# Where the tail of a matmul kernel's code lies: all supertiles inside the loop, the last emptied in halves, the last three chunks stored as one run per partition

## The chip, the cores and the metric

One core of one Trainium2 chip. The metric is the device time of one execution in microseconds (us); each kernel is executed several times, and medians are quoted with their range. The profile's span (first to last instruction) is about 1.7 us shorter than that time. All runs compared here are fast, at a granted TensorE clock of 0.995 or more.

## The reference

The depthwise kernel is 1x1, so the whole is a scale of each channel and a matrix product over 147,456 rows of 384 channels, in bf16:

```python
H = W = 384; C = 384; k = 1
out = out + xp[:, i:i+H, j:j+W, :] * dw[i, j][None, None, None, :]   # one (i, j) only
return jnp.einsum('bhwc,cd->bhwd', out, pw)                          # 384 x 384
```

## The kernel before

Rows are taken in 288 supertiles of 512. SyncE loads and stores chunks of one to ten supertiles. VectorE transposes a supertile in 32x32 blocks, TensorE multiplies it in 48 matmuls (four row tiles at a time) into one of two PSUM buffers, ScalarE empties the buffer into an output tile as bf16. The channel scale is folded into the weights at the start.

```python
head, tail = [[1, 1, 2, 2, 4]], [[6, 4], [3, 2, 1, 1, 1]]      # chunks, in supertiles
...
with nc.tensor.Fori(0, NS // 2 - 2, 1) as it:                  # 284 supertiles in the loop
    rv = nc.tensor.to_reg(it + 1)
    for s in range(2):
        supertile(s, rv)
supertile(0, NS // 2 - 1)                                      # three more as straight code
supertile(1, NS // 2 - 1)
supertile(0, NS // 2)
for ps, c0, c1 in ((1, 0, DS), (0, DS, D)):                    # the last: 256, then 128 columns
    ...                                                        # 48 matmuls each
```

So 480 instructions of straight code (matmuls with their weight loads) follow the loop. The last two supertiles are emptied by ScalarE and VectorE together, the last of them in two column parts. The two stores before the last write runs of 768 bytes; the very last store writes one run of 3072 bytes per partition:

```python
if t + 1 < NT:
    dst = of[512 * first : 512 * (first + L), :].rearrange("(q p j) d -> p q (j d)", q=4, p=P)
else:
    dst = of[512 * first :, :].rearrange("(m q) d -> m (q d)", q=4)
```

## Time and profile before

| | before |
|---|---|
| median, range | 577.61 us (577.1 to 577.85, 3 runs) |
| span of the profiled execution | 575.28 us |
| first emptying starts / last emptying is released | 9.85 / 569.56 us |
| last store issued / last landing seen by SyncE / end | 570.08 / 573.96 / 575.28 us |

TensorE sets the pace up to the last release; after that come a copy, a store and the closing of the program, 5.72 us together. I call this last stretch "release to end".

Two more views, which the prediction does not show. The first is the page's list of DMA queues (packets, MB, share of 16 engines' span); the second the SyncE queue in order of time near 512 us (start, duration of the issues, count):

```profile
q1 hardware_dynamic: 25924, 226.79, 98.0%
q8 instruction: 3, 0.05, 0.0%
q14 instruction: 9, 0.07, 0.0%
```

```profile
511.91 2.57 SPq L111 DMA_DIRECT2D X<-in_x_dram  x5
516.37 19.89 SPq L127 DMA_DIRECT2D out_dram<-O  x2
```

The DMA engines are 98% busy, and instructions travel through them too, on q8 and q14. Of the 19.89 us of the second SyncE row, the issue of one single store took 9.0 us by its record; most others take 0.33 to 0.5 us.

### The profile page before, as it was taken

The page shows a single profiled execution, that of the slowest core. Times are in us where ns is not written, and L with a number is a line of the kernel's source. Part 1 is how long each engine was busy: PE and PEld are TensorE (multiplying, and loading weights), DVE is VectorE, ACT ScalarE, POOL GpSimd, SP SyncE. Part 2 cuts the span into 40 slices and gives each one's busy share as a digit, 9 for nine tenths or more (in the row PEclk, how much of TensorE's full clock was granted, in tenths as well). Part 3 has the DMA queues.
Part 4 walks back from the last instruction along what each step waited for, and adds up shares of the span by engine and source line. Part 5 has one row for each costly group of instructions (what it writes and reads, how often), then busy time and mean ns, then how long its engine had stood idle before and what let it go on. Part 6 is the DMA issues. An engine that isn't in the chain of part 4 may idle for free.

```text
span 575.3 us, 29802 instructions
## 1 busy us (share of the span) xinstructions
PE 567.2 (99%) x13919; PEld 415.8 (72%) x13919; DVE 509.9 (89%) x584; ACT 418.2 (73%) x297; POOL 1.7 (0%) x8
## 2 busy tenths in 40 slices
PE   8999999999999999999999999999999999999995
PEld 5777777777777777777777777777777777777774
DVE  6999999999999999999999999999999999999994
ACT  6777777777777777777777777777777777777774
POOL 1000000000000000000000000000000000000000
PEclk9999999999999999999999999999999999999999
DMA  8999999999999999999999999999999999998876
GB/s 344 429 399 428 425 415 428 428 430 409 376 411 419 374 399 430 397 390 389 432 398 389 397 429 388 389 401 432 387 394 410 423 390 391 409 402 320 369 282 227
DMA packets 25938, 226.92 MB, mean 394 GB/s; under 512 B 1221, under 2 KB 5702, under 8 KB 22086
## 3 DMA queue, kind: packets, MB, share of 16 engines
q1 hardware_dynamic: 25924, 226.79, 98.0%
q8 instruction: 3, 0.05, 0.0%
q14 instruction: 9, 0.07, 0.0%
q10 hardware_dynamic: 2, 0.00, 0.0%
HBM read 113.54 MB, written 113.25 MB: 394 GB/s over the span
## 4 chain that ended last, share of the span: by engine, by line
PE 98%; ACT 0%; DVE 0%; issue 0%; POOL 0%; POOLq 0%; SPq 0%
PE ps L162 97%; PE ps L181 0%; ACT w_r L292 0%; PE ps L241 0%; DVE O L322 0%; PE ps L212 0%; POOL zero L253 0%; POOL warm L252 0%; POOLq L355 0%; PE ps L196 0%; SPq L99 0%
## 5 line engine op out<-in xcount | busy, mean ns | idle before, releaser
L162 PE MATMUL ps<-w_r,T 32*128 32x384 bf16 x13776 | 559.8, 321 | 0.9 <-ACT w_r L292 0.9
L279 DVE STREAM_TRANSPOSE T<-X 128x384 uint32<-128x384 uint32 x576 | 505.9, 879 | 54.4
L325 ACT CAST O<-ps 128x1536 bf16<-128x1536 f32 x289 | 413.0, 1429 | 148.3 <-PE ps L162 147.7
L162 PEld LDWEIGHTS ps<-w_r,T 32*128 32x128 bf16 x13776 | 411.6, 93 | 149.1 <-issue 1.2
L292 ACT CAST w_r<-ps 128x768 bf16<-128x768 f32 x5 | 3.6, 820 | 1.9 <-PE ps L212 1.9
L181 PE MATMUL ps<-zero 32*128 32x384 bf16 x32 | 2.8, 517 | 1.4 <-POOL zero L253 1.4
L322 DVE CAST O<-ps 128x768 bf16<-128x768 f32 (+2 forms) x3 | 2.1, 691 | 1.4 <-PE ps L162 1.1
L297 DVE COPY dw_f<-ps 128x3 f32<-128x3 f32 x1 | 0.2, 160 | 3.0 <-PE ps L196 3.0
L212 PE MATMUL ps<-pw_n,sel_w 128*128 128x384 bf16 x12 | 2.7, 357 | 0.0
L181 PEld LDWEIGHTS ps<-zero 32*128 32x128 bf16 x32 | 1.1, 118 | 2.0 <-issue 1.7
L212 PEld LDWEIGHTS ps<-pw_n,sel_w 128*128 128x128 bf16 x12 | 1.0, 105 | 1.9 <-issue 0.7
L265 ACT ACT_TABLE_LOAD x1 | 1.3, 1283 | 1.5 <-SPq L99 1.5
L241 PE MATMUL ps<-w_r,T 32*128 32x256 bf16 (+1 forms) x96 | 2.2, 241 | 0.0
L241 PEld LDWEIGHTS ps<-w_r,T 32*128 32x128 bf16 x96 | 2.0, 93 | 0.2
L292 DVE CAST w_r<-ps 128x768 bf16<-128x768 f32 x1 | 1.0, 956 | 1.2 <-PE ps L212 1.2
L301 DVE TENSOR_SCALAR sel_w<-sel,dw_f 128x512 bf16<-128x512 bf16 x3 | 0.9, 347 | 0.1
L255 POOL TENSOR_SCALAR_AFFINE_SELECT sel<-ones 128x512 bf16<-128x512 bf16 x1 | 0.7, 735 | 0.1
L196 PEld LDWEIGHTS ps<-ones,dw_row 1*128 1x128 bf16 x3 | 0.3, 127 | 0.3 <-issue 0.2
L254 POOL MEMSET ones<- 128x512 bf16 x1 | 0.5, 528 | 0.0
L265 ACT COPY warm<-warm 128x1 f32<-128x1 f32 x2 | 0.3, 189 | 0.0
L253 POOL MEMSET zero<- 128x192 uint32 x1 | 0.3, 258 | 0.0
L196 PE MATMUL ps<-ones,dw_row 1*128 1x1 bf16 x3 | 0.3, 174 | 0.0
(5 smaller groups left out, 0.5 us busy)
## 6 DMA issues: line engine op xcount, KB each, us to landing
X<-in_x_dram SPq DMA_DIRECT2D x26, 3840.0 KB, 21.8
out_dram<-O SPq DMA_DIRECT2D x26, 3840.0 KB, 27.8
X<-in_x_dram SPq DMA_DIRECT2D x2, 1536.0 KB, 17.5
out_dram<-O SPq DMA_DIRECT2D x2, 1536.0 KB, 14.6
X<-in_x_dram SPq DMA_DIRECT2D x3, 768.0 KB, 7.5
out_dram<-O SPq DMA_DIRECT2D x3, 768.0 KB, 9.6
X<-in_x_dram SPq DMA_DIRECT2D x1, 2304.0 KB, 19.9
out_dram<-O SPq DMA_DIRECT2D x1, 2304.0 KB, 12.8
```

Of the source, the lines that this page charges most:

```text
L162: mm = nc.tensor.matmul(PS[s][:, q, :D], lhsT=Ts[s][32 * q : 32 * q + 32, b, par::2], rhs=w_r[32 * q : 32 * q + 32, b, par, :], start=(b = ...
L181: nc.tensor.matmul(PS[0][:, i % 4, :D], lhsT=zero[32 * (i % 4) : 32 * (i % 4) + 32, 0:P], rhs=zero[32 * (i % 4) : 32 * (i % 4) + 32, :], s ...
L196: mm = nc.tensor.matmul(PS[1][:, k, D : D + 1], lhsT=dw_row[:, P * k : P * k + P], rhs=ones[0:1, 0, 0:1], start=True, stop=True,)
L212: mm = nc.tensor.matmul(w_ps(b)[:, r, :], lhsT=sel_w[:, b // 2, 2 * (b % 2) + r, :], rhs=pw_n[:, b // 2, :], start=True, stop=True,)
L241: mm = nc.tensor.matmul(PS[ps][:, q, : c1 - c0], lhsT=Ts[1][32 * q : 32 * q + 32, b, par::2], rhs=w_r[32 * q : 32 * q + 32, b, par, c0:c1] ...
L255: nc.gpsimd.affine_select(out=sel[:].rearrange("p (v r) (q w) -> p v r q w", v=2, q=4), in_=ones[:].rearrange("p (v r) (q w) -> p v r q w" ...
L265: c = nc.scalar.copy(warm[:, s + 1 : s + 2], warm[:, 0:1])
L279: ins = nc.vector.transpose(out=Tw[:, 3 * h : 3 * h + 3], in_=Xw[:, :, j, 96 * h : 96 * h + 96].rearrange("p k (b w) -> p b k w", w=32),)
L292: i = nc.vector.tensor_copy(out, in_) if e == 0 else nc.scalar.copy(out, in_)
L301: nc.vector.tensor_scalar_mul(sel_w[:, k], sel[:], dw_f[:, k : k + 1]).then_inc(s_sw)
L322: e = nc.vector.tensor_copy(Ov[:, nq:4, j, c0:c1], PS[ps][:, nq:4, : c1 - c0])
L325: a = nc.scalar.copy(Ov[:, 0:nq, j, c0:c1], PS[ps][:, 0:nq, : c1 - c0])
```

## The change

Its intent: a shorter program whose tail is the same code as its body, and longer runs in the last stores.

```diff
-            if t + 1 < NT:
+            if first + LONG < NS:                       # LONG = 3: the last three chunks
                 ...  # p-major load, 768-byte runs in the store
             else:
                 ...  # load in 768-byte runs, store in one 3072-byte run per partition
-        with nc.tensor.Fori(0, NS // 2 - 2, 1) as it:
+        with nc.tensor.Fori(0, NS // 2, 1) as it:
             rv = nc.tensor.to_reg(it + 1)
             for s in range(2):
                 supertile(s, rv)
-        supertile(0, NS // 2 - 1)
-        supertile(1, NS // 2 - 1)
-        supertile(0, NS // 2)
-        for ps, c0, c1 in ((1, 0, DS), (0, DS, D)):
-            ...
+            nq = 4
+            if jj + 1 == NS:
+                nq = 2
+                ...
+                e = nc.vector.tensor_copy(Ov[:, nq:4, j, :], PS[s][:, nq:4, :D])
+            a = nc.scalar.copy(Ov[:, 0:nq, j, :], PS[s][:, 0:nq, :D])
```

More of the change, by code (lines that the diff above doesn't have):

```diff
@@ L14 @@
 NR = 3
-DS = 256
+LONG = 3
 def _groups(n_super: int):
@@ L102, in load_x @@
             dst = Xs[g % NR][:, 4 * off : 4 * (off + L), :]
-            if t + 1 < NT:
-                src = xf[512 * first : 512 * (first + L), :].rearrange("(p s) c -> p (s c)", p=P)
+            rows = xf[512 * first : 512 * (first + L), :]
+            if first + LONG < NS:
+                src = rows.rearrange("(p s) c -> p (s c)", p=P)
                 dst = dst.rearrange("p s c -> p (s c)")
             else:
-                src = xf[512 * first :, :].rearrange("(a k q) c -> q a k c", k=4, q=4)
+                src = rows.rearrange("(a k q) c -> q a k c", k=4, q=4)
             if i == 0 and g >= NR:
@@ L116, in store @@
             src = Os[g % NR][:, 4 * off * D : 4 * (off + L) * D]
-            if t + 1 < NT:
-                dst = of[512 * first : 512 * (first + L), :].rearrange("(q p j) d -> p q (j d)", q=4, p=P)
+            rows = of[512 * first : 512 * (first + L), :]
+            if first + LONG < NS:
+                dst = rows.rearrange("(q p j) d -> p q (j d)", q=4, p=P)
                 src = src.rearrange("p (q e) -> p q e", q=4)
-                nc.sync.wait_ge(s_a[je % 2], je // 2 + 2)
-                if je >= NS - 2:
-                    nc.sync.wait_ge(s_d, 1)
-            else:
-                dst = of[512 * first :, :].rearrange("(m q) d -> m (q d)", q=4)
-                nc.sync.wait_ge(s_a[1], NS // 2 + 2)
-                nc.sync.wait_ge(s_d, 3)
+            else:
+                dst = rows.rearrange("(m q) d -> m (q d)", q=4)
+            nc.sync.wait_ge(s_a[je % 2], je // 2 + 2)
+            if je + 1 == NS:
+                nc.sync.wait_ge(s_d, 1)
             nc.sync.dma_start(dst, src).then_inc(s_o[g % NR], 16)
@@ L225 @@
                 supertile(s, rv)
-        supertile(0, NS // 2 - 1)
-        supertile(1, NS // 2 - 1)
-        supertile(0, NS // 2)
-        for ps, c0, c1 in ((1, 0, DS), (0, DS, D)):
-            for b in range(NB):
-                for par in range(2):
-                    for q in range(4):
-                        if par == 0 and q == 0:
-                            if ps == 1 and b in (0, 3):
-                                nc.tensor.wait_ge(s_t[1][b // 3], NS // 2)
-                            if b == 0:
-                                nc.tensor.wait_ge(s_a[ps], NS // 2 + (ps == 0))
-                                if ps == 0:
-                                    nc.tensor.wait_ge(s_d, 1)
-                        mm = nc.tensor.matmul(
-                            PS[ps][:, q, : c1 - c0],
-                            lhsT=Ts[1][32 * q : 32 * q + 32, b, par::2],
-                            rhs=w_r[32 * q : 32 * q + 32, b, par, c0:c1],
-                            start=(b == 0 and par == 0),
-                            stop=(b == NB - 1 and par == 1),
-                            tile_position=(32 * q, 0),
-                        )
-            mm.then_inc(s_pe)
         nc.gpsimd.memset(warm[:], 0.0).then_inc(s_seed)
@@ L312 @@
                 nc.scalar.wait_ge(s_o[g % NR], 16 * sum(map(len, groups[g % NR : g : NR])))
-            if jj + 2 < NS:
-                parts = [(s, 0, D, 4, 2 * jj + 2)]
-            elif jj + 2 == NS:
+            nq = 4
+            if jj + 1 == NS:
+                nq = 2
                 nc.vector.wait_ge(s_o[g % NR], 16 * sum(map(len, groups[g % NR : g : NR])))
-                parts = [(s, 0, D, 2, 2 * jj + 2)]
-            else:
-                parts = [(1, 0, DS, 2, 2 * jj + 1), (0, DS, D, 2, 2 * jj + 2)]
-            for ps, c0, c1, nq, v in parts:
-                if nq < 4:
-                    e = nc.vector.tensor_copy(Ov[:, nq:4, j, c0:c1], PS[ps][:, nq:4, : c1 - c0])
-                    e._wait_ge(s_pe, v)
-                    e.then_inc(s_d)
-                a = nc.scalar.copy(Ov[:, 0:nq, j, c0:c1], PS[ps][:, 0:nq, : c1 - c0])
-                a._wait_ge(s_pe, v)
-                a.then_inc(s_a[s])
+                e = nc.vector.tensor_copy(Ov[:, nq:4, j, :], PS[s][:, nq:4, :D])
+                e._wait_ge(s_pe, 2 * jj + 2)
+                e.then_inc(s_d)
+            a = nc.scalar.copy(Ov[:, 0:nq, j, :], PS[s][:, 0:nq, :D])
+            a._wait_ge(s_pe, 2 * jj + 2)
+            a.then_inc(s_a[s])
             if jj + 2 < NS:
```

## The prediction

> **What bounds the kernel now.** I read the page's busy shares first, then the chain that ended last, then the last 10 us in order of time, because the diff touches only the last five of 288 supertiles (512 rows each).
>
> ```profile
> PE 567.2 (99%) x13919; PEld 415.8 (72%) x13919; DVE 509.9 (89%) x584; ACT 418.2 (73%) x297; POOL 1.7 (0%) x8
> ...
> PE 98%; ACT 0%; DVE 0%; issue 0%; POOL 0%; POOLq 0%; SPq 0%
> ```
>
> TensorE is busy 99% of the span and carries 98% of the chain. One supertile is 48 matmuls of 384 columns. The ScalarE emptyings of consecutive supertiles start at 561.70, 563.65, 565.60 and 567.55 us in the trace: 1.95 us each, inside the loop and in the unrolled code after it alike. 288 x 1.95 = 561.6 us, and the change leaves all of it. What it can move is what lies after TensorE: 575.28 less the last release at 569.56, some 5.7 us, or 1% of the time. The timeline of that stretch (columns: start, duration, engine, line, operation, tiles, shape, count, idle before):
>
> ```profile
> 565.60 1.44 ACT L325 CAST O<-ps 128x1536 bf16<-128x1536 f32 x1 [0.51 <-PE ps L162]
> 567.07 3.35 SPq L127 DMA_DIRECT2D out_dram<-O  x3
> 567.16 2.17 PEld L241 LDWEIGHTS ps<-w_r,T 32*128 32x128 bf16 x96
> 567.32 2.19 PE L241 MATMUL ps<-w_r,T 32*128 32x256 bf16 x96
> 567.55 0.96 DVE L322 CAST O<-ps 128x768 bf16<-128x768 f32 x1 [1.07 <-PE ps L162]
> 567.55 0.80 ACT L325 CAST O<-ps 128x768 bf16<-128x768 f32 x1 [0.51 <-PE ps L162]
> 568.86 1.07 ACT L325 CAST O<-ps 128x512 bf16<-128x512 f32 x2 [0.51 <-PE ps L241]
> 568.86 1.12 DVE L322 CAST O<-ps 128x512 bf16<-128x512 f32 x2 [0.35 <-PE ps L241]
> ```
>
> The last supertile is computed as 256 and then 128 columns, so its first part is emptied (0.69 us on VectorE) while the second is computed; the second is released at 569.56 and costs another 0.42 us. The last copy ends at 569.98 and the last store is issued at 570.08. Then only DMA is left, as the SyncE queue's waits from 566 us on say:
>
> ```profile
> SPq L140 <- DMA out_dram<-O: 3.5, 1, 3.5
> ```
>
> That wait ends at 573.96; closing the program takes the other 1.31 us. The stretches after 571.5 us (sum, PE, PEld, DVE, ACT, POOL, clock, DMA share, GB/s) show how the DMA ends:
>
> ```profile
> 571.50:572.00 0.50, 0.00 (x0) 0.00 (x0) 0.00 (x0) 0.00 (x0) 0.00 (x0) 1.00 0.89 335
> 572.00:572.50 0.50, 0.00 (x0) 0.00 (x0) 0.00 (x0) 0.00 (x0) 0.00 (x0) 1.00 0.17 61
> 572.50:573.00 0.50, 0.00 (x0) 0.00 (x0) 0.00 (x0) 0.00 (x0) 0.00 (x0) 1.00 0.13 52
> 573.00:573.60 0.60, 0.00 (x0) 0.00 (x0) 0.00 (x0) 0.00 (x0) 0.00 (x0) 1.00 0.08 31
> ```
>
> From 572.0 on the share is 0.17, then 0.13: two to three of 16 engines are still moving. In the packet records, 13 engines write their 4-byte completion of the last store by 572.06, one at 572.35, the last two at 573.26 and 573.54. These two hold the end for about 1.2 us. Who delayed them? In the DMA view of 569.8 to 571.3 us:
>
> ```profile
> q1 hardware_dynamic: 475, 0.44, 88.0%
> q8 instruction: 1, 0.02, 5.6%
> q14 instruction: 1, 0.01, 1.3%
> ```
>
> Queue q8 has three packets in the whole execution, of 16384 B, at 12.8, 565.47 (961 ns) and 569.86 (1339 ns). The packets of the two late engines come at 33 ns spacing from about 571.75 on; up to the end of that fetch they stand still or come at 80 to 120 ns. A third engine lags for another reason (it worked off a backlog all through, landing the six-supertile store at 560.3 where the others did at 554.7) and has caught up: it is the 572.35.
>
> **What the Trainium skill says.** "Runtime: NRT & Kernel Launch", section "Instruction fetch mechanics": instructions stream in blocks of 16 KiB, 256 instructions, fetched by DMA while the engine runs. The trace agrees: between the q8 packets at 565.47 and 569.86 TensorE executed 278 matmuls and weight loads, and in some 550 us of looping there is no such packet. I therefore read q8 as TensorE's. "DMA: Bandwidth & Descriptors", section "Why a DMA increments its semaphore by 16 and not by 1": only all 16 mean landed, so the slowest engine sets a store's end; the 1.2 us agree. "ScalarE: Activation LUTs", section "What ACT_TABLE_LOAD costs": about 186 ns plus 0.833 ns per element; here 1536 elements took 1438 ns and 768 took 798 ns, the same slope of 0.833.
>
> **The change part by part.**
> (1) TensorE. The 480 unrolled instructions (five passes of 48 matmuls and 48 weight loads) go; two more loop turns take their place. The last release moves from 569.56 to 567.55 + 1.95 = 569.50: -0.06 us.
> (2) Last supertile. The two-part emptying becomes one after the matmuls: ScalarE 768 elements 0.80 us, VectorE 0.96 us (the rows at 567.55). The last copy ends at 569.50 + 0.96 = 570.46 instead of 569.98: +0.48 us. The store is issued at about 570.56.
> (3) Supertile before it: emptied whole by ScalarE, 1.44 instead of 0.96 us, so its store leaves at about 569.02 instead of 568.62. ScalarE is free at 568.99, before 569.50. Off the path.
> (4) Stores. The two stores before the last were 512 runs of 768 B, 32 to an engine at 33 ns = 1.06 us; now 8 to an engine at 117.5 ns (the last store's spacing) = 0.94 us. Saves 0.12 us an engine and store, mostly beside the wait for the last copy; it keeps the engines clear before the last store.
> (5) Loads. Two loads go from 3072 B to 768 B runs: +0.12 us an engine each, at 513 us; their data land by 533 and are needed after 560. Hidden, except that the backlogged engine carries up to 0.24 us to the end.
> (6) Fetches. With the unrolled code gone, the loop is followed by the end, so I expect neither late 16 KB fetch.
>
> Sum: in the kernel before, the 13 undisturbed engines' completions of the last store arrive at 572.23 to 572.41, which is 2.16 to 2.34 us after its issue. From 570.56 that gives 572.72 to 572.90. The backlogged engine: 572.35 + 0.24 for its packets and 0.4 for the receipt, 573.0. So the wait ends near 573.0 instead of 573.96: **-0.95 us**, the +0.48 included.
>
> **The rivals.**
> (a) The fetches stay or another comes: the jump from the loop to the program's end may fetch a block right at 569.5, and an 8 KB packet (q14, 570.75, 309 ns) was there before too. For it: the second fetch came when all code was nearly issued. Against it: 278 instructions between the two look like block after block of straight code. Then one engine lags as before, its packets begin later by up to 0.48 us, and the time is 577.5 to 578.1.
> (b) The copies are the bound: the emptying in halves adds its 0.48 us and the late engines cost nothing that matters. For it: the chain ends in the copies. Against it: the 3.5 us wait comes after them and ends on two engines. 578.1 us.
> (c) The backlogged engine becomes the last: the long runs save it 0.24 us, the loads take that away, and its lag differs from run to run. Then -0.5 us at most: 577.1.
> (d) The loop costs something at its turns. Against it: the cadence is 1.95 us in both codes. Nil.
>
> **Range and chances.** I give the sum about two in three, (a), (b) and (c) together one in three, at -0.95 and about -0.1 us: -0.7 to -0.85 on the median of 577.61. Prediction 576.8 us. Repeats of before spread over 0.75 us (577.1 to 577.85), and with rival (a) at the top the range is 576.0 to 577.9. Two per cent is 11.5 us, twice all that lies after TensorE, so faster or slower by that much is 0.005 each, 0.99 within.
>
> **What would show it.** Step 1: emptyings 1.95 us apart up to one starting near 569.50. Step 2: one VectorE copy of 768 elements at the end, last store issued near 570.56. Step 6: no q8 packet after 13 us; this is the step on which the sign hangs. Sum: SyncE's last wait 2.0 us instead of 3.5 (from about 570.95 to 573.0), the DMA share at 0.1 or more for half a microsecond at most after most engines stop. A q8 packet after 565 us, or single engines lagging by a microsecond without one, would make it wrong; so would a last store that lands over 2.5 us after its issue on all engines.

## The result

The changed kernel takes 576.25 us (575.67 to 577.12, 4 runs) against 577.49 us (577.1 to 577.85, 4 runs) of the kernel before. The ratio is 0.998, 95% interval 0.9963 to 0.9997. (A ratio is the mean time of one kernel's fast runs over that of the other's of the same rounds, so it is not quite the ratio of the medians.) Repeated later (e11_after_again) it was 576.52 against 577.44 us, ratio 0.9985 (0.9971 to 0.9998). A small gain, well inside the 2% that counts as the same.

The timeline of the last stretch of the changed kernel, columns as in the prediction:

```profile
565.37 1.44 ACT L296 CAST O<-ps 128x1536 bf16<-128x1536 f32 x1 [0.51 <-PE ps L162]
566.83 3.82 SPq L127 DMA_DIRECT2D out_dram<-O  x3
567.32 1.44 ACT L296 CAST O<-ps 128x1536 bf16<-128x1536 f32 x1 [0.51 <-PE ps L162]
569.27 0.80 ACT L296 CAST O<-ps 128x768 bf16<-128x768 f32 x1 [0.51 <-PE ps L162]
569.27 0.96 DVE L293 CAST O<-ps 128x768 bf16<-128x768 f32 x1 [3.02 <-DMA out_dram<-O]
```

The emptyings stay 1.95 us apart to the end; the last copy takes 0.96 us after the last release, where 0.42 us lay there before. (The releaser "DMA" named for VectorE is a wait that had long been met; SyncE's stores did not hold it.) SyncE's last wait, and the stretches after 571.5 us:

```profile
SPq L140 <- DMA out_dram<-O: 2.0, 1, 2.0
```

```profile
571.50:572.00 0.50, 0.00 (x0) 0.00 (x0) 0.00 (x0) 0.00 (x0) 0.00 (x0) 1.00 1.03 406
572.00:572.50 0.50, 0.00 (x0) 0.00 (x0) 0.00 (x0) 0.00 (x0) 0.00 (x0) 1.00 0.28 105
572.50:573.00 0.50, 0.00 (x0) 0.00 (x0) 0.00 (x0) 0.00 (x0) 0.00 (x0) 1.00 0.00 0
```

The wait fell from 3.5 to 2.0 us. After 572.5 us nothing moves: all 16 engines write their completions between 572.12 and 572.27. The long thin end of before is gone. The queues of the page:

```profile
q1 hardware_dynamic: 25900, 226.79, 98.0%
q14 instruction: 9, 0.07, 0.0%
q8 instruction: 1, 0.02, 0.0%
```

One q8 packet is left of three, at 12.39 us. So the two spans differ by 1.32 us, made up of three terms:

| term | before | after | difference |
|---|---|---|---|
| first emptying starts | 9.85 | 9.62 | -0.23 |
| first to last release (TensorE) | 559.71 | 559.65 | -0.06 |
| release to end | 5.72 | 4.69 | -1.03 |

The first is scatter: over all the traces below it starts anywhere from 9.38 to 10.46 us. In the last, the copy adds 0.53 us and the way from the store's issue to the end of the wait gives back 1.56 us (3.89 to 2.33).

One thing moved far from the end. SyncE near 512 us, and the stretch that follows (columns as above, DMA share and GB/s last), first before and then after:

```profile
517.00:531.00 14.00, 14.00 (x352) 10.29 (x348) 12.66 (x15) 10.42 (x8) 0.00 (x0) 1.00 0.80 315
```

```profile
511.67 14.51 SPq L112 DMA_DIRECT2D X<-in_x_dram  x5
526.22 9.80 SPq L127 DMA_DIRECT2D out_dram<-O  x2
```

```profile
517.00:531.00 14.00, 14.00 (x352) 10.26 (x344) 12.63 (x15) 10.42 (x8) 0.00 (x0) 1.00 0.41 144
```

With the last loads in 768-byte runs, the issues of two loads and of the next store took 8.4, 4.4 and 4.4 us, and the store left at 526.22 instead of 516.37. (e5_short_runs below, which undoes the new runs alone, issues its five loads in 2.57 us again.) The DMA share halved for 14 us. TensorE did not notice: 14.00 us busy in both.

### The profile page after: what moved, and what is told of

It is laid out like the page before. It is cut to its first block, busy times and chain, and to the rows that moved or that the text cites. A ratio compares the mean times of both kernels' runs of the same rounds, so it can differ in the third digit from the quotient of the medians.

```text
span 574.0 us, 29707 instructions
## 1 busy us (share of the span) xinstructions
PE 566.9 (99%) x13871; PEld 415.2 (72%) x13871; DVE 507.4 (88%) x582; ACT 418.7 (73%) x296; POOL 1.7 (0%) x8
## 4 chain that ended last, share of the span: by engine, by line
PE 98%; ACT 1%; DMA 0%; DVE 0%; issue 0%; POOL 0%; POOLq 0%; SPq 0%
PE ps L162 97%; PE ps L181 0%; DMA out_dram<-O 0%; ACT w_r L268 0%; ACT O L296 0%; DVE O L293 0%; PE ps L212 0%; POOL zero L229 0%; POOL warm L228 0%; POOLq L326 0%; PE ps L196 0%; SPq L99 0%
```

## The experiments

The theory: **straight code behind the loop makes TensorE fetch its instructions through the DMA engines (q8, 16 KB packets); a fetch in the last microseconds makes single engines late, and the last store waits for the slowest engine.** The main rival: the long runs of the last stores made the engines level.

The table gives all runs, read from their traces. "Late" is by how much the last completion in the packet records comes after the ninth of the last 16, "q8" the packets after 500 us. Where the last supertile is split in two parts (before, e2, e4, e6, e9), the last store is issued some 0.52 us after the release, in the others about 1.05 us or later (e7 and e10: in halves, 0.82 and 1.20 us): there a late engine has some 0.5 us more to catch up. So read "late" together with "release to end".

| run | q8 at | late, us | release to end, us | median, us (before beside it) | ratio |
|---|---|---|---|---|---|
| before | 565.47, 569.86 | 1.54 | 5.72 | 577.61 | |
| after | none | 0.08 | 4.69 | 576.25 (577.49) | 0.9980 |
| e1_unroll6 | 561.39, 566.36 | 0.31 | 4.92 | 576.47 (577.10) | 0.9987 |
| e1_unroll4 | 566.08 | 0.08 | 4.69 | 576.52 (577.10) | 0.9984 |
| e2_split_looped | 570.05 | 1.15 | 5.28 | 577.20 (577.10) | 0.9995 |
| e3_early | none | 0.09 | 4.69 | 577.27 (577.10) | 1.0001 |
| e4_long_only | 565.97, 571.65 | 1.45 | 5.64 | 577.32 (577.09) | 1.0008 |
| e5_short_runs | none | 0.07 | 4.69 | 576.32 (577.09) | 0.9980 |
| e6_split_more_code | 561.20, 567.38 | 0.51 | 4.60 | 576.47 (577.09) | 0.9989 |
| e7_two_stores | none | 0.09 | 4.55 | 576.37 (577.09) | 0.9987 |
| e8_act_whole | none | 0.08 | 5.11 | 576.89 (577.44) | 0.9988 |
| e9_split_shifted | 561.84, 566.19, 576.19 | 0.73 | 4.91 | 578.05 (577.44) | 1.0013 |
| e10_two_stores_again | none | 0.08 | 4.55 | 575.98 (577.44) | 0.9977 |
| e11_after_again | none | 1.57 | 6.28 | 576.52 (577.44) | 0.9985 |

The confidence intervals of the ratios are 0.0012 to 0.0017 to each side (0.0024 for e4_long_only), so most kernels are not told apart by time. The traces do that; each is one execution.

### e4_long_only and e5_short_runs: the two causes apart

The kernel before with the long runs alone, and the changed kernel with LONG undone:

```diff
# e4_long_only, against before
-            if t + 1 < NT:
+            if first + 3 < NS:      # loads and stores as in the change; TensorE's code and the emptying stay
# e5_short_runs, against after
-LONG = 3
+LONG = 1
```

> The kernel before with one part of the change alone: the last three chunks loaded and stored as in the changed kernel, 3072 bytes a run in the store. TensorE's code stays, so theory: q8 packets near 565.5 and 570 us as before, the late engines stay 0.8 to 1.2 us late, last wait 3.0 to 3.5 us, release to end 5.2 to 5.7 us. Rival 1 (the long runs made the engines level): last wait 1.9 to 2.2 us, release to end 4.2 to 4.4 us.

> The changed kernel with 768-byte runs for the two stores before the last, as before the change (the last one stays long). No late q8. Theory: the two stores cost each engine 0.12 us more, beside the wait for the last copy: last wait 1.9 to 2.2 us, release to end 4.7 to 4.9 us. Rival 1: single engines late again, last wait 2.5 us or more, release to end over 5.2 us.

The last wait of SyncE, e4_long_only first and e5_short_runs after it:

```profile
SPq L142 <- DMA out_dram<-O: 3.5, 1, 3.5
```

```profile
SPq L140 <- DMA out_dram<-O: 2.0, 1, 2.0
```

Long runs with the straight code: late. Short runs without it: level, and the same 4.69 us as with long runs. The rival falls. (In time, on the same chip: 577.32 us, 576.30 to 579.78 in 4 runs, against 576.32 us, 575.85 to 576.51 in 4 runs.) The two runs differ in the emptying too, not in the straight code alone; e1 and e6 below tell these apart. In the packet records of e4_long_only one can follow the engine: a 16384-byte packet runs from 571.65 to 572.60; the eight 3072-byte packets of the last store that follow in one line start at 572.58, the first two taking 335 and 295 ns instead of 121, and their completion at 573.90 is the last of all. The records name no engine; the line is made by each packet starting where the one before ends. Behind the first fetch, in the same way, the next two packets of 1536 bytes take 178 and 885 ns, where the others take about 67 (161 and 871 in the kernel before, 164 and 876 in e1_unroll4). So a fetch can cost its engine 1.9 us or more, twice the length of its own packet.

### e1_unroll4 and e1_unroll6: straight code in the changed kernel

```diff
-        with nc.tensor.Fori(0, NS // 2, 1) as it:
+        with nc.tensor.Fori(0, NS // 2 - 3, 1) as it:       # e1_unroll4: - 2
             ...
+        for turn in (NS // 2 - 2, NS // 2 - 1, NS // 2):     # e1_unroll4: the last two
+            for s in range(2):
+                supertile(s, turn)
```

> The changed kernel with its last six supertiles as straight code again (576 instructions) and nothing else altered. Theory (late fetches of TensorE's code delay single DMA engines): q8 packets of 16 KB come back after the loop, the second near 567.5 to 568 us; one engine then ends the last store 0.5 to 1.2 us after the others and SyncE's last wait is 2.4 to 3.2 us instead of 1.94; the time is 0.4 to 1.2 us above the changed kernel. Rival 1 (the long runs of the last stores are what made the engines level): wait stays at 1.9 to 2.1 us, time as the changed kernel, q8 or not. Rival 2 (it is the start of the program or its scatter): no relation to q8.

> As the run with six, but four supertiles as straight code (384 instructions). Theory: one late q8 packet, near 565.3 us as the first one of the kernel before; an engine loses up to 1.8 us there but has the gaps between the last stores to make it up, so the last wait is 1.9 to 2.4 us, a smaller loss than with six. If a second packet comes near 569 to 570 us the wait is 2.5 us or more. Rival 1: 1.94 us and no loss.

The q8 packets came back with the straight code, as many as expected. With four supertiles the fetch at 566.08, 4.0 us before the last release, cost nothing in the end. With six the second came at 566.36, 3.4 us before the release and at least 1.1 us earlier than I expected; one engine was 0.31 us late and the wait 2.17 us. My range of 0.4 to 1.2 us of loss was a miss: release to end grew by 0.23 us. The direction is the theory's: straight code alone, in a kernel that empties as the changed one does, brings the packets back, and with six supertiles a late engine. That its place and not its amount decides is argued from these runs, which change both.

### e2_split_looped: the split kept, less straight code

```diff
-        with nc.tensor.Fori(0, NS // 2 - 2, 1) as it:
+        with nc.tensor.Fori(0, NS // 2 - 1, 1) as it:
             ...
-        supertile(0, NS // 2 - 1)
-        supertile(1, NS // 2 - 1)
         supertile(0, NS // 2)
```

> The kernel before with its two-part last supertile and its 768-byte stores, but with two of the unrolled turns... that is supertiles 284 and 285 moved into the loop (288 instructions of straight code left instead of 480). Theory: at most one q8 packet after the loop, near 568 to 570 us or none; without a packet the late engines are gone, the last store is issued about 0.5 us earlier than in the changed kernel relative to TensorE's end, and the time is 0.3 to 0.5 us below the changed kernel (span near 573.5); with a packet at 568 to 570 us one engine is about 1 us late and the time is near the kernel before. Rival 1 (long runs did it): last wait stays at 3.2 to 3.6 us with or without the packet, time as before.

From the DMA view of its 568 to 573 us, and its last wait:

```profile
q8 instruction: 1, 0.02, 1.2%
q14 instruction: 1, 0.01, 0.4%
```

```profile
SPq L140 <- DMA out_dram<-O: 3.1, 1, 3.1
```

The one packet left fell at 570.05, as badly as possible, and two engines were late (completions at 573.46 and 573.74, the others by 572.66). It alone would not have told theory and rival apart.

### e3_early: the same straight code in front of the loop

```diff
+        for turn in (1, 2, 3):
+            for s in range(2):
+                supertile(s, turn)
-        with nc.tensor.Fori(0, NS // 2, 1) as it:
-            rv = nc.tensor.to_reg(it + 1)
+        with nc.tensor.Fori(0, NS // 2 - 3, 1) as it:
+            rv = nc.tensor.to_reg(it + 4)
```

> The changed kernel with six supertiles as straight code in front of the loop instead of behind it: the same amount of fetching, at another place. Theory: two or three q8 packets before 25 us and none after, last wait 1.9 to 2.1 us, time within 0.3 us of the changed kernel. Rival 2 (straight code as such costs TensorE time): the emptyings of the first six supertiles come more than 1.95 us apart and the time rises as with the code at the end.

The end is as good as expected (4.69 us, no late fetch; q8 at 12.75, 19.03 and 26.03). But the time is that of the kernel before. The emptyings of the first supertiles show where it went:

```profile
13.28 1.44 ACT L299 CAST O<-ps 128x1536 bf16<-128x1536 f32 x1 [0.51 <-PE ps L162]
15.80 1.44 ACT L299 CAST O<-ps 128x1536 bf16<-128x1536 f32 x1 [1.08 <-PE ps L162]
...
19.70 1.44 ACT L299 CAST O<-ps 128x1536 bf16<-128x1536 f32 x1 [0.51 <-PE ps L162]
22.80 1.44 ACT L299 CAST O<-ps 128x1536 bf16<-128x1536 f32 x1 [1.67 <-PE ps L162]
```

Two steps are 2.52 and 3.10 us instead of 1.95, together 1.72 us. TensorE's row for 7 to 28 us says what it waited for:

```profile
L162 PE MATMUL ps<-w_r,T 32*128 32x384 bf16 x472 | 19.9, 321 | 1.9 <-issue 1.2 <-ACT w_r L271 0.7
```

"issue" 1.2 us: no semaphore held it. I read this as TensorE waiting for its own instructions while the loads saturate the DMA engines; TensorE starts again at 15.24 and 21.44 us, some 1.4 us after a q8 packet ends each time (13.79 and 20.04), which speaks for it; but no run delayed a fetch alone, and the third packet (26.03) has no such gap. Rival 2 was right about the time here, though not at the end of the program, where TensorE ran at 1.95 us in straight code too.

### e8_act_whole: is the copy on the path?

```diff
-                e = nc.vector.tensor_copy(Ov[:, nq:4, j, :], PS[s][:, nq:4, :D])   # and its wait
             a = nc.scalar.copy(Ov[:, 0:nq, j, :], PS[s][:, 0:nq, :D])               # nq stays 4
```

> The changed kernel with the last supertile emptied whole by ScalarE, 1.44 us, instead of in halves. Theory: with no late engine the copy lies wholly on the path, so release to end is 4.69 + 0.48 = 5.15 to 5.2 us and the last wait stays 1.9 to 2.0 us. Rival (the DMA sets the end whatever the issue): 4.7 to 4.9 us with a shorter wait.

Release to end is 5.11 us, 0.42 more than the changed kernel's 4.69, and the wait is 1.93 us as before. The copy itself is 0.48 us longer; without VectorE's semaphore SyncE issues 0.02 instead of 0.09 us after it, which is the rest. With level engines the copy lay on the path in full.

### e7_two_stores and e10_two_stores_again: the last store in halves

```diff
             if je + 1 == NS:
+                nc.sync.dma_start(dst[:, : 2 * D], src[:, : 2 * D]).then_inc(s_o[g % NR], 16)
                 nc.sync.wait_ge(s_d, 1)
+                dst, src = dst[:, 2 * D :], src[:, 2 * D :]
             nc.sync.dma_start(dst, src)...
```

> The changed kernel with the last store cut in two of 1536 bytes a partition: ScalarE's half is issued when ScalarE's copy is done, VectorE's half after its own. Theory: the first half is issued about 0.16 us earlier than the whole was, the second at most 0.25 us later and moves half as much (0.5 instead of 0.94 us an engine), so the last landing is 0.1 to 0.25 us earlier: release to end 4.45 to 4.6 us. Rival: the issue of the second, 0.35 us behind the first, eats it all: 4.65 to 4.8 us.

> The run with the last store in two halves once more, beside the changed kernel on the same chip. Release to end 4.5 to 4.6 us (it was 4.55), median 0.1 to 0.2 us below the changed kernel, which may drown in the scatter of some 0.5 us between executions.

```profile
SPq L142 <- DMA out_dram<-O: 1.6, 1, 1.6
```

The stores are issued at 570.55 and 570.93, the last landing is 0.14 us earlier relative to the release, twice the same (4.55 us). On the second chip (e10) it took 575.98 us against 576.52 for the changed kernel, ratio to before 0.9977 (0.9963 to 0.9991); on the first, 576.37 us (e7). The traces support 0.14 us; by time alone it is not told apart from the changed kernel.

### e6_split_more_code and e9_split_shifted: the split with its fetches moved away

If only the place of the fetch matters, the split of before (last copy 0.42 us after the release instead of 0.96) with more straight code should win.

```diff
# e6_split_more_code, against e4_long_only
-        with nc.tensor.Fori(0, NS // 2 - 2, 1) as it:
+        with nc.tensor.Fori(0, NS // 2 - 3, 1) as it:
             ...
+        supertile(0, NS // 2 - 2)
+        supertile(1, NS // 2 - 2)
# e9_split_shifted, against e6_split_more_code: the warm-up matmuls written out, eight more of them
-            with nc.tensor.Fori(0, n, 1) as _:
-                for i in range(8):
+            for i in range(8 * n):
...
-        idle_work(2)
+        idle_work(3)
```

> The kernel before (two-part last supertile) with the long runs of the change and with MORE straight code: seven supertiles behind the loop (672 instructions) instead of five. By the q8 times of the earlier runs a block boundary lies some 230 to 250 instructions after the loop's end and every 256 after it, so the two fetches should come near 559 to 560.5 and 564.5 to 565.5 us, more than 4 us before TensorE's last release, where a fetch did no harm with four supertiles. Theory: all 16 engines complete within 0.3 us, last wait 1.9 to 2.2 us, the stretch from the last release to the end 4.1 to 4.3 us (changed kernel 4.69, before 5.72), time 0.3 to 0.6 us under the changed kernel. Rival 1 (straight code behind the loop as such, or the split, makes the engines uneven): wait 3 us or more and the time of the kernel before.

> The run with more straight code, with some 40 instructions more in front of the loop (the warm-up matmuls written out, eight more of them), so that the block boundaries lie about 0.85 us earlier after the loop. Theory: q8 near 560.5 and 565.5 to 566.5 us relative to a last release near 570.1, all 16 engines complete within 0.3 us, release to end 4.1 to 4.3 us, that is 0.4 to 0.6 us less than the changed kernel, and the median 0.3 to 0.6 us below it if the start is not delayed. Rival: an engine is still 0.4 us late, 4.5 to 4.7 us.

More straight code did make the end shorter: 4.60 us against 5.64 of e4_long_only, which differs by those two supertiles alone. So it is not the split emptying alone that makes engines late. But the second fetch came at 567.38, later than I worked out; 6.2 us after the first, where 256 instructions at 1.95 us per 96 make 5.2 us. It cost 0.51 us of lateness and ate most of the split's gain. The shifted version was worse: 4.91 us (its late engine met an 8 KB packet of q14 as well, see the next run), and a third q8 packet at 576.19, after the last instruction of the program at 575.04. In three of its five executions the time exceeded the span by 2.05, 2.45 and 3.35 us, in those of all the other experiments by 1.67 to 1.88. What comes after the span belongs to no row of the profile; I can only say that the fetch lies there. Both are misses as kernels.

### e11_after_again: the changed kernel once more

> The changed kernel once more, unedited, as the reference for the other three on the same chip. Release to end 4.65 to 4.75 us, last wait 1.9 to 2.0 us, no q8 packet after 13 us, median 576.0 to 576.6 us; where two executions differ it is in when the first emptying starts (9.6 to 10.5 us so far).

The profiled execution was the slowest of five (577.47 us), and its end is not what I expected: no q8 packet, and yet one engine 1.57 us late.

```profile
SPq L140 <- DMA out_dram<-O: 3.6, 1, 3.6
```

```profile
571.80:572.30 0.50, 0.00 (x0) 0.00 (x0) 0.00 (x0) 0.00 (x0) 0.00 (x0) 1.00 0.99 393
572.30:572.80 0.50, 0.00 (x0) 0.00 (x0) 0.00 (x0) 0.00 (x0) 0.00 (x0) 1.00 0.22 86
572.80:573.30 0.50, 0.00 (x0) 0.00 (x0) 0.00 (x0) 0.00 (x0) 0.00 (x0) 1.00 0.09 37
573.30:574.00 0.70, 0.00 (x0) 0.00 (x0) 0.00 (x0) 0.00 (x0) 0.00 (x0) 1.00 0.05 22
```

This is a second way to be late. In every trace, for the store landing near 515 to 517 us (by the increments of its semaphore), one engine is 9.7 to 11.2 us behind the ninth and a second one 0.6 to 2.9 us. They use the pauses of the last 30 us to catch up. For the store whose median landing is near 566 us, the last engine was 0.9 us behind in the first profile of the changed kernel and 2.3 us here; with 2.3 the pauses that follow are too short, and its packets run without a break to the last completion at 573.99. A smaller fetch is among them: an 8192-byte packet of q14, another queue of kind instruction, from 571.076 to 571.385. This engine's packet before it ends at 571.080, and the two behind it take 198 and 294 ns instead of about 118. That is some 0.55 us of the 1.57; the backlog is the rest. Such a packet is in every trace (in the first profile of the changed kernel at 569.16, in a pause of all engines), so q8 is not the whole of late fetching. So the gain of the change is not safe in each execution, and part of the scatter between 575.67 and 577.47 us comes from this.

## Why the prediction was right

**The time.** Predicted 576.8 us in 576.0 to 577.9; measured 576.25 and 576.52. The predicted change of -0.8 us was measured as -1.24 and -0.92. (The weighing itself, two thirds of -0.95 and one third of -0.1, gives -0.67 and not -0.7 to -0.85.) The traced difference of 1.32 us holds 0.23 us of luck at the start.

**Step 1** (TensorE, -0.06): 559.71 to 559.65 us. Right.

**Step 2** (+0.48 by the last copy): the copy ends 0.96 us after the release instead of 0.42. The predicted sum of the two steps holds, and e8_act_whole shows that the copy is on the path in full. Rival (b) saw this part and missed the larger one. (Of the formula cited for ScalarE the slope holds; the constant is 158 ns here, 1438 - 1536 x 0.833, and not 186.)

**Step 3** (off the path): ScalarE is free at 568.76, before 569.27. Right.

**Step 4** (stores, 0.12 us an engine, mostly hidden): e5_short_runs has the same 4.69 us, so all of it is hidden.

**Step 5** (loads, hidden, up to 0.24 us on the backlogged engine): hidden they were, but this is the step that was mis-sized. What the shorter runs did was to hold up SyncE's issues by some 17 us, 8.4 + 4.4 + 4.4, where before one issue of 9.0 us stood, and to keep most engines idle for 14 us. It did not reach the end; ScalarE's emptyings are never over 1.95 us apart. I looked at the cost of a packet and not at that of an issue.

**Step 6** (no late fetch) carried the sign, and it held: no q8 after 13 us, all 16 engines within 0.15 us, the wait 1.94 us where 2.0 was predicted. e4_long_only and e5_short_runs show that this, and not the runs, is the gain; from issue to the end of the wait it was 2.33 us where I had 2.44. One reading on the way was wrong: I put both late engines down to the second fetch, and their slow packets to the time up to its end. It ends at 571.195, and slow packets go on to 571.76. From 571.05 on there are 74 packets of 768 bytes: ten are the lagging engine's, the other 64 are all 32 of the last store but one on each late engine. One row begins at 571.179, where the second fetch ends; the other at 571.056, where the 8 KB packet of q14 ends (571.059), and that engine was about 1 us behind already in the store landing at 568.6, after the first fetch. So both 16 KB fetches cost, and the change removed both.

**Rival (a)** is what happens in e4_long_only and e2_split_looped. **Rival (c)** was under-sized: I gave it at most half of the gain (577.1 us); e11_after_again is such an execution, at 577.47 us, with nothing gained, 1.0 us by the backlog and some 0.55 by the q14 packet on the same engine.

**Open.** In e2_split_looped, too, two engines are late with one 16 KB packet and one 8 KB packet (q14) nearby; that each delays one, as in the kernel before, fits but is not settled there. No run moved the q14 packet. Why the packets behind a fetch are slow is open. Why one engine falls behind all through the program is open too, and why an issue of SyncE can take 9 us: that it waits for room on the lagging engine would fit, but nothing here tests it.

## What to carry to other kernels

When a program ends in DMA, look at the completion of each engine and not at the bandwidth: one late engine of 16 sets the end. Straight code behind a long loop is fetched through the same engines just when they matter; keep the tail inside the loop, or see to it that its fetch falls early, and measure where it falls. No safe distance was found: a fetch 4.0 us before the last release cost nothing in e1_unroll4, but after fetches 4.1 us (before) and 3.9 us (e9_split_shifted) ahead of it an engine that then met an 8 KB packet was still late. Compare the tails inside one trace (release to end) when the effect is smaller than the scatter of the start.

## What the Trainium skill lacked or had wrong

- "Runtime: NRT & Kernel Launch", section "Instruction fetch mechanics", calls the cost of crossing a 16 KiB boundary mostly hidden and says that kernels prefer full unrolling. The runs differ at both ends: a 16384-byte packet of about 0.95 us on an engine made the last store 1.45 us late (e4_long_only), and straight code in front of the loop cost TensorE 1.72 us (e3_early), while the loop's 144 turns cost nothing (emptyings 1.95 us apart). What the section warns of is a branch out of the two pages at hand; this loop of 192 instructions gave no q8 packet in some 550 us.
- "DMA: Bandwidth & Descriptors" names a row for instruction refill among the rings of the same engines (section "Queues, rings and completion order"), but not how long such a packet holds one: 0.88 to 1.44 us for 16 KB beside a store, and as much as 0.9 us more in the packets behind it. It gives row 14 for the refill; the 16 KB blocks that follow TensorE's straight code are on q8 here, and q14 has packets of 8 KB.
- None of the pages read here has that one issue on the SyncE queue can take 4.4 to 9.0 us (up to 13.9 near the start) instead of 0.33 to 0.5, nor by how much one engine can lag behind the other fifteen at full load: some 10 us here.
